# Attention and two FFNs on one core: attention by blocks of 256 tokens, in an order planned task by task

## The chip, the core and the metric

The kernel runs on one core of a Trainium2 chip. Its time is the device time of one execution in microseconds (us). The core has five engines with a queue of their own each: TensorE (PE, its weight loads shown as PEld), VectorE (DVE), ScalarE (ACT), GpSimd (POOL) and SyncE (SP), whose queue issues most DMAs. An engine works through its queue in order; what it needs from another engine it waits for at the instruction concerned.

## What is computed

Attention over 2 batches, 8 heads, 768 tokens and heads of 64, then two FFNs on the 1536 x 512 result, all in float32:

```python
scores = scale * np.matmul(q, k.transpose(0, 1, 3, 2))
is_sink = pos[None, :] < int(n_sink)                  # n_sink = 4
rel = pos[:, None] - pos[None, :]
in_window = (rel >= 0) & (rel < int(window))          # window = 128
scores = np.where(is_sink | in_window, scores, -1000000000.0)
a = np.exp(scores - np.max(scores, axis=-1, keepdims=True))
x = np.matmul(a / (np.sum(a, axis=-1, keepdims=True) + 1e-09), v)   # then (B, H, S, D) -> (B*S, H*D)
h = x @ w_in                                          # FFN 0: 512 -> 2048
g = np.where(h >= 1, h, np.where(h <= -1, 0.0, (h + 1) ** 2 / 4))
x = g @ w_out                                         # 2048 -> 512
h = x @ moe2_w_in                                     # FFN 1
out = np.maximum(h, 0.0) ** 2 @ moe2_w_out
```

The weights arrive as 64-bit floats and are turned into 32-bit numbers by bit operations on the chip.

## The kernel before

**Attention.** A unit of work (`UNITS`, L36) is a batch `b`, a block `j` of 256 tokens and a pair `c` of heads: 2 x 3 x 4 = 24 units. Because of the window, a unit needs the keys of its own block and, for j > 0, the last 128 keys of the block before and the 4 sink keys. Its steps are: load q, k, v for two pairs (`Loads.load`); copy the block-before keys by DMA on SP and the sink keys on POOL (`keys_before`); transpose k and q on PE and copy them out on DVE (`turn`); scores on PE for 128 rows of both heads, then mask, scale and minimum on DVE, then the exponential with its sum on ACT (`scores`, twice, `u` = 0 and 1); the reciprocal on DVE and the product with it on POOL, and for j > 0 the sink columns on POOL (`norm`); transposes of the weights on PE, copied by ACT (`turn_p`, twice; `turn_s` for the sink columns); the products with the values on PE, and the result split into a rounded high part (ACT) and the rest (DVE) in `x` (`values_of`).

**The FFNs.** Each product is done as three fp32r matmuls (`SPLIT`: high x high, high x low, low x high). The 2048 hidden columns of an FFN are 16 chunks of 128. A pass (`PASSES`, from `CUTS`, L48) holds two to four chunks; a step is one pass over some tokens: per chunk 12 matmuls for the hidden values (`hidden`, L175) and the activation on ACT, DVE and POOL, then four outputs of three matmuls per chunk (`outs`, L209), which DVE adds to an accumulator (L232, L234). A weight chunk comes in two halves (`part`, L121 to L130): two instructions on ACT, four on DVE, one on ACT, one on POOL, with one temporary buffer. Converted chunks stand in a ring of nine, six of which exist while attention runs.

**Order.** The order of `UNITS` is batch, then two pairs, then the three blocks of tokens, then the pairs. Each step of a unit has a number in `ORDER` (L44): unit index plus that number is its place in one list, which `fast_path` sorts. Into the same list go the weight conversions (`JOBS`), fillers on PE (`warm_pe`) and six FFN steps of 256 tokens (`STEPS`, L47): three of pass 0 (two chunks), three of pass 1 (three chunks). The scheduler of the language then picks, for each engine, what its model of time finds ready, with the list as priority. Behind attention its buffers are given to three more weight chunks, more hidden buffers (`G1`) and more PSUM banks, and the steps go on with 512 tokens (256 where a rest is left), always with the next conversions between the pieces (`Plan.job`).

Of the kernel before, what the change touches and what calls it, by code (L numbers as in the profile page):

```python
# [17 lines left out]
P = 128  # L18
# [14 lines left out]
AGAIN = 5, 2, 2, 2, 2, 2, 2, 2, 2, 1, 1, 1, 1, 1, 1, 1, 1  # L33
VB, KB = 3, 4
# [6 lines left out]
RING, EARLY = 9, 6  # L41
G0, G1 = 4, 6
LINE, BOTTOM, TOP = 2048, 26656, 229344
PSF, SCB, TPB, TXB, AVB = 2, 1, 1, 2, 1  # L44
JOBS = [4.00, 4.01, 4.50, 4.51, 5.05, 5.06, 5.58, 5.59, 6.63, 6.64, 6.81, 6.82, 7.15, 7.16, 7.67, 7.68, 8.20, 8.21, 8.44, 8.45, 8.68, 8.69, 9.47, 9.48]
ORDER = dict(
    q=-1.149, k=-2.190, v=-1.001, s0=-0.630, s1=0.512, t=-0.860, n=0.752, x0=1.240, xs=1.996, x1=1.174, a=2.080,  # L47
)  # L48
STEPS = [(13.70, (0, 0, 256)), (13.50, (0, 256, 256)), (17.60, (0, 512, 256)), (21.70, (1, 0, 256)), (21.20, (1, 256, 256)), (22.00, (1, 512, 256))]
CUTS = ((0, 2, 5, 8, 12, 16), (0, 4, 8, 12, 16))  # L50
# [6 lines left out]
def f32(ap):  # L57
    return ap.bitcast(F32)

# [27 lines left out]
class Weights:  # L87
# [20 lines left out]

    def part(self, key, h, tmp):
        nc, r = self.nc, self.raw.pop((key, h))  # L110
        if h == 0:
            pool = self.ring[self.turn % len(self.ring)]
            self.turn += 1
            self.split[key] = pool.tile([P, 2, 2 * E], F32R, tag="w", name=f"w_{key[0]}_{key[1]}")
        w = self.split[key][:, :, h * E : (h + 1) * E]
        nm = f"{key[0]}_{key[1]}_{h}"
        x = tmp.tile([P, E], F32, tag="wx", name=f"wx_{nm}")
        y = tmp.tile([P, E], F32, tag="wy", name=f"wy_{nm}")
        xi, yi = x.bitcast(I32), y.bitcast(I32)
        lo, hi = r[:, :, 0], r[:, :, 1]  # L120
        nc.scalar.activation(x, f32(hi), AF.Abs, scale=65536.0)  # L121
        nc.scalar.activation(yi, lo.bitcast(U32), AF.Copy, scale=2.0**-29)  # L122
        nc.vector.tensor_scalar(x, x, 2.0, None, ALU.max)  # L123
        nc.vector.tensor_scalar(xi, xi, 3, None, ALU.logical_shift_left)  # L124
        nc.vector.scalar_tensor_tensor(  # L125
            xi, hi, -(1 << 31), xi, ALU.bitwise_and, ALU.bitwise_or
        )
        nc.vector.tensor_tensor(xi, xi, yi, ALU.add)  # L128
        nc.scalar.copy(w[:, 0], x)  # L129
        nc.gpsimd.tensor_tensor(w[:, 1], x, f32(w[:, 0]), ALU.subtract)  # L130


class Ffn:
# [28 lines left out]
    def hidden(self, st, i):  # L162
# [3 lines left out]
        w = self.weights.split[key]  # L166
        x = self.x
        sl = slice(st["off"], st["off"] + nt)
        if i == 0:
            st["g"] = []  # L170
        h = self.bank(f"h_{nm}")[:, :nt]
        n = 0
        for c in range(4):
            for a, b in SPLIT:
                nc.tensor.matmul(  # L175
                    h, w[:, a, c * P : (c + 1) * P], x[:, b, c, sl], start=n == 0, stop=n == 11
                )
                n += 1
        g = po["g"].tile([P, 2, nt], F32R, tag="g", name=f"g_{nm}")
        u = po["tmp"].tile([P, nt], F32, tag="u", name=f"u_{nm}")  # L180
        if ffn == 0:
            t = po["tmp"].tile([P, nt], F32, tag="t", name=f"t_{nm}")
            nc.scalar.activation(u, h, AF.Relu, bias=self.half, scale=0.5)  # L183
            nc.vector.scalar_tensor_tensor(t, u, 1.0, u, ALU.min, ALU.mult)  # L184
            nc.vector.tensor_tensor(u, h, t, ALU.max)  # L185
            nc.scalar.copy(g[:, 0], u)  # L186
            nc.gpsimd.tensor_tensor(g[:, 1], u, f32(g[:, 0]), ALU.subtract)  # L187
        else:
            t = po["tmp"].tile([P, nt], F32, tag="t", name=f"t_{nm}")
            nc.scalar.activation(u, h, AF.Relu)  # L190
            nc.vector.scalar_tensor_tensor(t, h, 0.0, u, ALU.max, ALU.mult)  # L191
            nc.scalar.copy(g[:, 0], t)  # L192
            nc.gpsimd.tensor_tensor(g[:, 1], t, f32(g[:, 0]), ALU.subtract)  # L193
        st["g"].append(g)

    def outs(self, st, ob, part=slice(0, E)):
        nc = self.nc
        ffn, off, nt, chunks = st["ffn"], st["off"], st["nt"], st["chunks"]
        width = nt if ffn == 0 else part.stop - part.start
        o = self.bank(f"o_{st['nm']}_{ob}")[:, :width]  # L200
        n, m = 0, 3 * len(chunks)
        for key, g in zip(chunks, st["g"]):
            w = self.weights.split[key]
            for i, j in SPLIT:
                if ffn == 0:
                    lhs, rhs = w[:, i, E + ob * P : E + (ob + 1) * P], g[:, j, :]
                else:
                    lhs, rhs = g[:, i, ob * P : (ob + 1) * P], w[:, j, E:][:, part]
                nc.tensor.matmul(o, lhs, rhs, start=n == 0, stop=n == m - 1)  # L209
                n += 1  # L210
# [35 lines left out]
class Plan:  # L246
# [3 lines left out]
    def __init__(self, ffn, weights, wtmp):  # L250
# [11 lines left out]
        self.at = 0  # L262
# [68 lines left out]
class Attention:  # L331
# [17 lines left out]
    def sinks(self, b):  # L349
        nc, v = self.nc, self.loads.src["v"]  # L350
        raw = self.po["pt"].tile([P, 512], F32, tag="pt", name=f"vsr_{b}")
        raw = raw[:96].rearrange("p (h d) -> p h d", h=H)
        vs = self.po["vs"].tile([96, H, D], F32R, tag="vs", name=f"vs_{b}")
        nc.gpsimd.memset(raw, 0.0)
        for base in (0, 32, 64):
            for e in range(2):
                nc.sync.dma_start(
                    raw[base + e * NS : base + (e + 1) * NS, e::2, :],
                    v[b, e::2, 0:NS, :].rearrange("h t d -> t h d"),
                )  # L360
        nc.vector.tensor_copy(vs, raw)
        nc.vector.tensor_tensor(vs[64:96], raw[64:96], f32(vs[64:96]), ALU.subtract)
        self.vs[b] = vs

    def keys_before(self, b, j, c):
        nc = self.nc
        kt = self.po["k"].tile([P, 5, SLOT], F32, tag="k", name=f"k_{b}_{j}_{c}")
        if j > 0:
            old = self.kt[b, j - 1, c]
            nc.sync.dma_start(kt[:, 0, :P], old[:, 2, :P])  # L370
            nc.gpsimd.tensor_copy(
                kt[:, 0:2, P:], old[:, 1, P:].unsqueeze(1).broadcast_to([P, 2, NS])
            )
        self.kt[b, j, c] = kt

    def turn(self, b, j, c):
        nc, po, kt = self.nc, self.po, self.kt[b, j, c]
# [12 lines left out]
        for i in range(banks):  # L390
            blocks = slice(4 * i // banks, 4 * (i + 1) // banks)
            nc.vector.tensor_copy(kt[:, 1:, :P][:, blocks], ps[i][:, blocks])
        if j == 0:
            nc.gpsimd.tensor_copy(kt[:, 1, P:], kt[:, 1, :NS])
        self.st[b, j, c] = dict(nm=f"{b}_{j}_{c}")

    def scores(self, b, j, c, u):
# [6 lines left out]
        ps = [banks[:, e, :wid] for e in range(2)]  # L404
# [5 lines left out]
        if u == 0:  # L410
            st["p"] = [
                po["p"].tile([P, 2, WIN], F32, tag="p", name=f"p_{st['nm']}_{i}") for i in range(2)
            ]
            st["sm"] = po["sm"].tile([P, 3, 2, 2], F32, tag="sm", name=f"sm_{st['nm']}")
        s, sm = st["p"][u][:, :, :wid], st["sm"]
        mask = self.masks[min(2 * j + u, 2)][:, :wid]
        for e in range(2):
            nc.vector.tensor_tensor_reduce(  # L418
                s[:, e], ps[e], mask, -SCALE, 3.0e38, ALU.add, ALU.min, sm[:, 0, u, e : e + 1]
            )  # L420
        for e in range(2):
            nc.scalar.activation(  # L422
# [4 lines left out]
    def norm(self, b, j, c):  # L427
        nc, st = self.nc, self.st[b, j, c]
        sm = st["sm"]
        nc.vector.tensor_scalar(sm[:, 1], sm[:, 1], 1.0e-9, None, ALU.add)  # L430
        nc.vector.reciprocal(sm[:, 2], sm[:, 1])  # L431
        if j > 0:
            st["sp"], st["stt"] = self.sink_p[c % 2], self.sink_t[c % 2]
        for u in range(2):
            wid = P if j + u == 0 else WIN
            s = st["p"][u][:, :, :wid]
            r = sm[:, 2, u].unsqueeze(2).broadcast_to([P, 2, wid])
            nc.gpsimd.tensor_tensor(s, s, r, ALU.mult)  # L438
# [388 lines left out]
```

## Time and profile before

| | |
|---|---|
| runs, median (lowest to highest) | 666.81 us (665.79 to 667.2), 3 runs |
| the profiled execution | 669.3 us; span from first to last instruction 667.5 us |
| mean granted clock of PE in it | 0.994 |
| busy, of the span | PE 645.5, DVE 425.1, ACT 324.4, POOL 296.1 us |
| first score matmul, last value pass done | 8.93 us, 173.3 us |
| last matmul begun or running until | 662.7 us |

A matmul's end in the profile is modelled; the distance between the starts of two neighbours is what it cost where they stand close. An engine's idle time counts only where the chain of waits runs through it. Granted clock 1.00 is 2.4 GHz, 0.50 is 1.2 GHz.

### The profile page before, as it was taken

Reading aid. Unit: us, or ns where it says so; the run is one execution under the profiler, and the core shown is the slowest. Engines: PE = TensorE matmul, PEld = TensorE weight load, DVE = VectorE, ACT = ScalarE, POOL = GpSimd, SP = SyncE. Lnnn points to the kernel's source line nnn. Section 1 sums busy time; section 2 is a strip of 40 time slices with the busy share of each in tenths; the row PEclk is TensorE's granted clock in tenths of the full one; section 3 lists DMA queues with packets and bytes.
Section 4 is the critical chain, followed back from the end, with each engine's and each line's share of the span. In section 5 each row is a group of like instructions: output and inputs, shape, how many; then the busy total and the mean of one; then the engine's idle time right before and its main releaser. Section 6 shows DMA issues by size and latency. Waiting matters only on the chain.

```text
span 667.5 us, 9576 instructions
## 1 busy us (share of the span) xinstructions
PE 645.5 (97%) x3400; PEld 524.7 (79%) x3400; DVE 425.1 (64%) x885; ACT 324.4 (49%) x702; POOL 296.1 (44%) x302
## 2 busy tenths in 40 slices
PE   8888999999999999999999999999999999999997
PEld 7554677888888888877888878888888888888886
DVE  5688898966488887867776865664566356222221
ACT  2688877665454545445545554453444354122110
POOL 1365667546053535354346576353335343233111
PEclk9999899999999999999999989999999999999999
DMA  4846453110322222232312221321123020000111
GB/s 106 212 123 168 118 136 96 25 36 1 127 64 66 93 78 81 64 93 66 95 64 64 63 64 32 95 80 47 54 72 95 32 64 1 0 1 0 64 63 70
DMA packets 64345, 47.95 MB, mean 72 GB/s; under 512 B 40096, under 2 KB 58784, under 8 KB 64288
## 3 DMA queue, kind: packets, MB, share of 16 engines
q1 hardware_dynamic: 63456, 46.72, 24.1%
q8 instruction: 29, 0.48, 0.3%
q10 hardware_dynamic: 832, 0.52, 0.2%
q14 instruction: 28, 0.23, 0.1%
HBM read 43.04 MB, written 3.15 MB: 69 GB/s over the span
## 4 chain that ended last, share of the span: by engine, by line
PE 45%; DVE 5%; POOL 2%; ACT 2%; issue 1%; POOLq 0%; DVEq 0%
PE o L209 24%; PE h L175 21%; DVE t L184 1%; POOL x L220 1%; DVE wx L125 1%; POOL g L187 1%; DVE u L185 1%; POOL w L130 1%; DVE wx L123 1%; DVE wx L128 1%; DVE wx L124 0%; ACT u L183 0%; ACT g L186 0%; ACT wx L121 0%; ACT wy L122 0%
## 5 line engine op out<-in xcount | busy, mean ns | idle before, releaser
L175 PE MATMUL h<-x,w 128*128 128x512 f32 (+1 forms) x1272 | 272.7, 371 | 0.0
L175 PEld LDWEIGHTS h<-x,w 128*128 128x128 f32 x1272 | 223.8, 188 | 43.4 <-issue 1.2
L209 PE MATMUL o<-g,w 128*128 128x512 f32 (+1 forms) x696 | 143.8, 359 | 3.8 <-POOL g L187 2.0
L130 POOL TENSOR_TENSOR w<-wx,w 128x512 fp32r<-128x512 f32 x64 | 83.1, 1299 | 141.0 <-ACT w L129 133.5
L209 PEld LDWEIGHTS o<-g,w 128*128 128x128 f32 x696 | 116.6, 190 | 27.2 <-POOL g L187 3.9
L209 PE MATMUL o<-w,g 128*128 128x512 f32 (+1 forms) x588 | 132.7, 385 | 0.0
L209 PEld LDWEIGHTS o<-w,g 128*128 128x128 f32 x588 | 108.9, 188 | 22.1
L193 POOL TENSOR_TENSOR g<-t,g 128x512 fp32r<-128x512 f32 x48 | 64.1, 1335 | 100.5 <-ACT g L192 84.0
L234 DVE TENSOR_TENSOR acc<-o,acc 128x512 f32<-128x512 f32 (+1 forms) x105 | 58.3, 578 | 53.7 <-PE o L209 53.7
L187 POOL TENSOR_TENSOR g<-u,g 128x512 fp32r<-128x512 f32 (+1 forms) x58 | 69.0, 1192 | 52.7 <-ACT g L186 26.4
L129 ACT CAST w<-wx 128x512 fp32r<-128x512 f32 x64 | 39.9, 624 | 106.1 <-DVE wx L128 88.6
L123 DVE TENSOR_SCALAR wx<-wx 128x512 f32<-128x512 f32 x64 | 39.1, 611 | 60.9 <-ACT wx L121 60.7
L191 DVE SCALAR_TENSOR_TENSOR t<-h,u 128x512 f32<-128x512 f32 x48 | 33.1, 689 | 60.6 <-ACT u L190 34.4
L438 POOL TENSOR_TENSOR p<-p,sm 128x520 f32<-128x520 f32 (+1 forms) x48 | 49.5, 1052 | 44.5 <-DVE sm L431 44.5
L190 ACT ACTIVATE u<-h 128x512 f32<-128x512 f32 x48 | 28.6, 596 | 63.4 <-PE h L175 63.3
L125 DVE SCALAR_TENSOR_TENSOR wx<-wraw,wx 128x512 int32<-128x512 int32 x64 | 58.2, 910 | 1.2
L121 ACT ACTIVATE wx<-wraw 128x512 f32<-128x512 f32 x64 | 42.7, 668 | 32.3 <-POOL w L130 26.9
L422 ACT ACTIVATE p<-p,sm 128x260 f32<-128x260 f32 (+1 forms) x96 | 46.9, 491 | 22.5 <-DVE sm L418 22.4
L184 DVE SCALAR_TENSOR_TENSOR t<-u 128x512 f32<-128x512 f32 (+1 forms) x58 | 42.0, 726 | 18.6 <-ACT u L183 18.4
L128 DVE CUSTOM_DVE_ANT_0 wx<-wx,wy 128x1024 uint16<-128x1024 uint16 x64 | 50.1, 783 | 1.0
L122 ACT ACTIVATE wy<-wraw 128x512 int32<-128x512 uint32 x64 | 42.8, 668 | 6.9 <-DVE wx L128 6.9
L186 ACT CAST g<-u 128x512 fp32r<-128x512 f32 (+1 forms) x58 | 31.6, 546 | 27.9 <-DVE u L185 27.1
(72 smaller groups left out, 561.7 us busy)
## 6 DMA issues: line engine op xcount, KB each, us to landing
wraw<-in_moe_w_in_dram SPq DMA_DIRECT2D x32, 512.0 KB, 3.6
wraw<-in_moe_w_out_dram SPq DMA_DIRECT2D x32, 512.0 KB
vr<-in_v_dram SPq DMA_DIRECT2D x24, 128.0 KB, 2.3
qr<-in_q_dram SPq DMA_DIRECT2D x22, 128.0 KB, 2.8
kr<-in_k_dram SPq DMA_DIRECT2D x22, 128.0 KB, 2.8
out_dram<-acc SPq DMA_DIRECT2D x10, 256.0 KB, 2.0
k<-k SPq DMA_DIRECT2D x16, 64.0 KB, 2.5
qr<-in_q_dram SPq DMA_DIRECT2D x4, 64.0 KB
```

Of the source, the lines that this page charges most:

```text
L123: nc.vector.tensor_scalar(x, x, 2.0, None, ALU.max)
L125: nc.vector.scalar_tensor_tensor(xi, hi, -(1 << 31), xi, ALU.bitwise_and, ALU.bitwise_or)
L128: nc.vector.tensor_tensor(xi, xi, yi, ALU.add)
L130: nc.gpsimd.tensor_tensor(w[:, 1], x, f32(w[:, 0]), ALU.subtract)
L175: nc.tensor.matmul(h, w[:, a, c * P : (c + 1) * P], x[:, b, c, sl], start=n == 0, stop=n == 11)
L184: nc.vector.scalar_tensor_tensor(t, u, 1.0, u, ALU.min, ALU.mult)
L187: nc.gpsimd.tensor_tensor(g[:, 1], u, f32(g[:, 0]), ALU.subtract)
L193: nc.gpsimd.tensor_tensor(g[:, 1], t, f32(g[:, 0]), ALU.subtract)
L209: nc.tensor.matmul(o, lhs, rhs, start=n == 0, stop=n == m - 1)
L234: self.nc.vector.tensor_tensor(dst, o, dst, ALU.add)
L422: nc.scalar.activation(s[:, e], s[:, e], AF.Exp, bias=sm[:, 0, u, e : e + 1], scale=-1.0, accum_out=sm[:, 1, u, e : e + 1],)
L438: nc.gpsimd.tensor_tensor(s, s, r, ALU.mult)
```

## The change

- `UNITS` now runs batch, block, pair: all four pairs of 256 tokens stand together, and a block's predecessor is four units back.
- Every step of attention, of the weight conversion and of the FFN steps is cut into functions that issue instructions of one engine each (`keys_load`, `keys_sink`, `turn`, `turn_copy`, `scores`, `least`, `powers`, `norm`, `weigh`, `sink_cols`, `turn_p`, `turn_p_copy`, `turn_s`, `turn_s_copy`, `turn_s_low`, `values_of`, `rows_high`, `rows_low`; `parts`; `hidden_parts`, `out_parts`). The instructions themselves are the same. A hidden product is two tasks of six matmuls that begin when all four pairs are there.
- A `Planner`, run when the program is built, simulates the engines with a price per kind of task (`COST`) and gives each task a time: always the task that can start first, and among equals the lowest key (`KEYS`, `STEPS`, `LOADS`, `PARTS`). The tasks are issued in that order within `manual_schedule()`, which keeps each engine's order inside the region; where later instructions fall among them stays the scheduler's.
- Ten FFN steps of 256 tokens are in the plan instead of six, of passes of three chunks each: `CUTS` of FFN 0 becomes (0, 3, 6, 10, 13, 16). Pass 2 then holds chunks 6 to 9. Six chunks are converted in the plan, as before.
- Fillers on PE go into gaps of the plan ahead of the first FFN matmul only (`warm_gaps`).
- Buffers: v 5 instead of 3, keys 6 instead of 4, hidden 7 instead of 4, both accumulators at fixed places; the room comes from a smaller scratch for DMA descriptors (`DMA_SCRATCH`).

```diff
-UNITS = [
-    (b, j, g * GRP + c)
-    for b in range(B) for g in range(NC // GRP) for j in range(3) for c in range(GRP)
+UNITS = [(b, j, c) for b in range(B) for j in range(3) for c in range(NC)]
-STEPS = [(13.70, (0, 0, 256)), (13.50, (0, 256, 256)), (17.60, (0, 512, 256)), (21.70, (1, 0, 256)), (21.20, (1, 256, 256)), (22.00, (1, 512, 256))]
-CUTS = ((0, 2, 5, 8, 12, 16), (0, 4, 8, 12, 16))
+STEPS = [
+    (0, 0, 10.09), (0, 256, 12.27), (1, 0, 9.77), (0, 512, 3.39), (1, 256, 14.42),
+    (0, 768, 18.80), (1, 512, 19.48), (0, 1024, 24.08), (1, 768, 42.06), (1, 1024, 21.07),
+]
+CUTS = ((0, 3, 6, 10, 13, 16), (0, 4, 8, 12, 16))
+START = 8700.0
+LAG = dict(PE=53, ACT=33, DVE=33, POOL=78, SP=40)
+COST = dict(
...
+    e=("ACT", 994, 1100, 0), es=("ACT", 780, 880, 0), xc=("ACT", 492, 587, 0), xxc=("ACT", 375, 467, 0),
...
+class Planner:
...
+    def run(self):
...
+        while len(order) < len(self.tasks):
+            best = None
+            for e, tasks in ready.items():
+                for t in tasks:
+                    at = self.starts(t, free)
+                    if at is not None:
+                        c = (max(at, idle[e]), t.key, t)
+                        if best is None or c[:2] < best[:2]:
+                            best = c
...
+            order.append(t)
...
+def warm_gaps(order, nc, ident, psf):
+    out, last, begun = [], START, False
+    for t in order:
+        if t.engine == "PE":
+            begun = begun or t.kind in ("mm", "m1")
+            count = int((t.start - last - 250) / 225)
+            if count > 0 and not begun:
+                out.append(lambda n=len(out), c=count: warm_pe(nc, ident, psf, f"c{n}", c))
+            last = t.start + t.step
+        out.append(t.emit)
+    return out
...
-            for _, _, f, args in sorted(events, key=lambda ev: ev[:2]):
-                if f == calls["s0"] and args == UNITS[0]:
-                    with tc.manual_schedule(engines={mybir.EngineType.DVE}):
-                        f(*args)
-                        masks.rest()
-                else:
-                    f(*args)
-            plan.flush()
+            at.mask_rest = masks.rest
+            with tc.manual_schedule():
+                order = fast_plan(at, ffn, weights, plan.stage, plan.wtmp)
+                for emit in warm_gaps(order, nc, at.ident, psf):
+                    emit()
```

## Rows read from the trace of the kernel before

**Rows 1.** The page, part 1: engine, busy us (share of the span) x instructions.

```profile
PE 645.5 (97%) x3400; PEld 524.7 (79%) x3400; DVE 425.1 (64%) x885; ACT 324.4 (49%) x702; POOL 296.1 (44%) x302
```

**Rows 2.** Windows: stretch, length, busy us by engine, granted clock, DMA share, GB/s.

```profile
core 0: us, PE busy (x) PEld busy (x) DVE busy (x) ACT busy (x) POOL busy (x), PEclk, DMA share, GB/s
...
9.00:40.80 31.80, 26.77 (x198) 18.91 (x198) 22.61 (x85) 20.42 (x66) 11.27 (x21) 1.00 0.65 163
40.80:100.00 59.20, 53.08 (x399) 37.42 (x397) 52.49 (x166) 47.96 (x142) 37.23 (x54) 0.97 0.56 143
100.00:173.30 73.30, 72.08 (x582) 58.88 (x580) 53.41 (x164) 46.92 (x139) 39.80 (x57) 1.00 0.14 37
...
395.60:662.70 267.10, 267.06 (x1181) 221.23 (x1181) 122.45 (x184) 96.33 (x164) 98.37 (x75) 0.99 0.14 46
```

**Rows 3.** The chain of waits, late: start us, us, what.

```profile
406.83 10.88 PE h L175 x48
```

**Rows 4.** Groups from 9 to 173.3 us: busy us, mean ns; idle before.

```profile
L407 PE MATMUL s<-k 64*128 64x260 f32 (+1 forms) x192 | 33.1, 417 | 6.6 <-DVE sm L418 5.8 <-DVE k L392 0.5 <-issue 0.2
L453 PE MATMUL tx<-ident,p 128*128 128x128 f32 x176 | 30.0, 283 | 1.3 <-POOL p L438 0.9 <-DMA wraw<-in_moe_w_in_dram 0.3
L175 PE MATMUL h<-x,w 128*128 128x256 f32 (+1 forms) x181 | 27.4, 295 | 0.0
L209 PE MATMUL o<-g,w 128*128 128x256 f32 x180 | 27.3, 294 | 1.0 <-DVE acc L232 0.8 <-DVE u L185 0.2
...
L491 PE MATMUL av<-pt,vr 128*64 128x128 f32 (+1 forms) x256 | 24.8, 326 | 1.6 <-ACT pt L457 0.8 <-DVE x L494 0.7
...
L385 PE MATMUL tp<-ident,kr 128*128 128x128 f32 x46 | 10.3, 296 | 0.4 <-DMA kr<-in_k_dram 0.4
...
L184 DVE SCALAR_TENSOR_TENSOR t<-u 128x256 f32<-128x256 f32 x15 | 7.9, 537 | 4.1 <-ACT u L183 4.0
...
L185 DVE TENSOR_TENSOR u<-h,t 128x256 f32<-128x256 f32 x15 | 6.2, 419 | 0.5
```

**Rows 5.** Timeline of PE, 100 to 215 us: start, us, instruction, count.

```profile
151.92 0.28 PE L491 MATMUL av<-sink_t,vs 96*128 96x256 f32 x1
152.13 1.09 PE L491 MATMUL av<-pt,vr 128*64 128x256 f32 x12
153.15 0.66 PE L453 MATMUL tx<-ident,p 128*128 128x128 f32 x4
153.56 1.08 PE L209 MATMUL o<-g,w 128*128 128x256 f32 x7
154.57 0.71 PE L407 MATMUL s<-k 64*128 64x260 f32 x4
155.21 0.65 PE L453 MATMUL tx<-ident,p 128*128 128x128 f32 x4
...
157.09 2.40 PE L209 MATMUL o<-g,w 128*128 128x256 f32 x18
159.33 0.28 PE L491 MATMUL av<-sink_t,vs 96*128 96x256 f32 x1
```

**Rows 6.** Timeline of PE, 0 to 60 us.

```profile
40.79 0.60 PE L175 MATMUL h<-x,w 128*128 128x256 f32 x3
```

**Rows 7.** Timeline of ACT, 0 to 45 us.

```profile
23.48 0.37 ACT L493 CAST x<-av 128x256 fp32r<-128x256 f32 x1
```

**Rows 8.** Timeline of POOL, 160 to 310 us; 17 like rows of L130 lie between.

```profile
182.38 1.30 POOL L130 TENSOR_TENSOR w<-wx,w 128x512 fp32r<-128x512 f32 x1 [15.60 <-ACT w L129]
...
305.55 1.30 POOL L130 TENSOR_TENSOR w<-wx,w 128x512 fp32r<-128x512 f32 x1
```

**Rows 9.** Timeline of the DMA queue SP, 120 to 310 us.

```profile
173.40 0.37 SPq L101 DMA_DIRECT2D wraw<-in_moe_w_in_dram  x1
```

**Rows 10.** Windows in the thin stretch; columns as in rows 2.

```profile
65.00:70.00 5.00, 3.20 (x18) 1.88 (x19) 4.11 (x16) 4.81 (x15) 3.19 (x4) 0.88 0.39 112
70.00:72.00 2.00, 2.00 (x11) 1.59 (x11) 1.43 (x7) 1.57 (x6) 1.05 (x4) 0.50 0.00 0
```

More of the change, by code (lines that the diff above doesn't have):

```diff
@@ L58, in f32, with __init__, add, starts @@
     return ap.bitcast(F32)
+class Hold:
+    def __init__(self, pool):
+        self.pool, self.left, self.end = pool, 0, 0.0
+class Task:
+    def __init__(self, kind, key, emit, after, takes, uses):
+        self.kind, self.key, self.emit = kind, key, emit
+        self.engine, self.step, self.took, self.extra = COST[kind]
+        self.after = [t for t in after if t is not None]
+        self.takes, self.uses = takes, uses
+        self.next = []
+        self.start = self.end = None
+class Planner:
+    def __init__(self, slots, start):
+        self.slots, self.begin, self.tasks = slots, start, []
+    def add(self, kind, key, emit, after=(), takes=(), uses=()):
+        t = Task(kind, (key, len(self.tasks)), emit, after, list(takes), list(uses))
+        for h in t.uses:
+            h.left += 1
+        for d in t.after:
+            d.next.append(t)
+        self.tasks.append(t)
+        return t
+    def starts(self, t, free):
+        at = t.ready
+        need = {}
+        for h in t.takes:
+            need[h.pool] = need.get(h.pool, 0) + 1
+        for pool, n in need.items():
+            if len(free[pool]) < n:
+                return None
+            at = max(at, sorted(free[pool])[n - 1] + LAG[t.engine])
+        return at
+    def run(self):
+        free = {pool: [0.0] * n for pool, n in self.slots.items()}
+        ready = {e: [] for e in LAG}
+        idle = {e: self.begin for e in LAG}
+        dma, gps = self.begin, [(0.0, 0.0)]
+        for t in self.tasks:
+            t.wait, t.ready = len(t.after), self.begin
+            if not t.wait:
+                ready[t.engine].append(t)
+        order = []
+        while len(order) < len(self.tasks):
[7 more added lines that the diff above has]
+                            best = c
+            assert best, [(e, [t.kind for t in tasks]) for e, tasks in ready.items()]
+            at, _, t = best
+            ready[t.engine].remove(t)
+            step, took = t.step, t.took
+            if t.engine == "DVE" and t.extra:
+                more = sum(max(0.0, min(b, at + took) - max(a, at)) for a, b in gps[-3:]) * t.extra
+                step, took = step + more, took + more
+            t.start = at
+            idle[t.engine] = at + step
+            if t.engine == "SP":
+                dma = max(at + step + 900, dma) + t.extra
+                t.end = dma + 1100
+            else:
+                t.end = at + took
+            if t.engine == "POOL":
+                gps.append((at, t.end))
+            for h in t.takes:
+                free[h.pool].remove(min(free[h.pool]))
+            for h in t.uses:
+                h.left -= 1
+                h.end = max(h.end, t.end)
+                if not h.left:
+                    free[h.pool].append(h.end)
+            order.append(t)
+            for x in t.next:
+                x.wait -= 1
+                same = x.engine == t.engine and t.engine != "SP"
+                lag = (0 if t.engine == "PE" else 34) if same else LAG[x.engine]
+                end = t.start + t.step if same and t.engine == "PE" else t.end
+                x.ready = max(x.ready, end + lag)
+                if not x.wait:
+                    ready[x.engine].append(x)
+        return order
@@ L196, in outs, with hidden, out_parts @@
+        return ops + [("gc", high), ("gl", low)]
+    def hidden(self, st, i):
+        for _, f in self.hidden_parts(st, i):
+            f()
+    def out_parts(self, st, ob):
+        n = len(st["chunks"])
+        s = {}
+        return [
+            ("mm", lambda a=a: self.out_mm(st, ob, slice(0, E), a, min(a + 2, n), s))
+            for a in range(0, n, 2)
+        ] + [("ad", lambda: self.out_add(st, ob, slice(0, E), s["o"]))]
     def outs(self, st, ob, part=slice(0, E)):
+        s = {}
+        self.out_mm(st, ob, part, 0, len(st["chunks"]), s)
+        self.out_add(st, ob, part, s["o"])
@@ L197, in outs, with out_mm @@
+    def out_mm(self, st, ob, part, lo, hi, s):
         nc = self.nc
-        ffn, off, nt, chunks = st["ffn"], st["off"], st["nt"], st["chunks"]
+        ffn, nt, chunks = st["ffn"], st["nt"], st["chunks"]
         width = nt if ffn == 0 else part.stop - part.start
[L200 to L203, printed above, removed]
+        if lo == 0:
+            s["o"] = self.bank(f"o_{st['nm']}_{ob}")[:, :width]
+        for n in range(lo, hi):
+            w, g = self.weights.split[chunks[n]], st["g"][n]
@@ L261, in __init__ @@
         self.left = [NT] * len(PASSES)
-        self.at = 0
+        for ps, _, _ in STEPS if begun else ():
+            self.left[ps] -= HALF
+        self.at = 4 * EARLY if begun else 0
         self.pend = []
@@ L349, in sinks @@
     def sinks(self, b):
[L350 to L360, printed above, removed]
@@ new lines, in fast_plan @@
+def fast_plan(at, ffn, weights, stage, wtmp):
+    line = Planner(SLOTS, START)
+    units = at.plan(line)
+    plan_ffn(line, ffn, weights, stage, wtmp, units)
+    return line.run()
+def warm_gaps(order, nc, ident, psf):
[9 more added lines that the diff above has]
+    return out
```

525 lines of the change are left out of this document (353 added, 172 removed).

## The prediction

> **What bounds the kernel now.** I read the page's busy times first, then the stages as windows, then the order on TensorE, then the instruction groups of the attention stage. TensorE (PE) is busy for 97% of the span [rows 1], so only time in which PE is badly filled can be won. The windows say where that is [rows 2]: from 395.6 to 662.7 us PE is busy without a break, and the chain there runs through matmuls alone, 48 of 512 columns in 10.88 us, 0.2267 us each [rows 3]. From 9.0 to 173.3 us, the attention stage, the three windows show 5.0, 6.1 and 1.2 us of open idle time. The rest of the bad filling is hidden in "busy", because the modelled end of a matmul covers short waits. So I price PE's own work there by start-to-start intervals in dense places [rows 5]: a score step (four passes) takes 0.64 us (154.57 to 155.21), a transpose of 128 columns 0.41/4 = 0.1025 us (153.15 to 153.56), a pass of the values 1.02/12 = 0.085 us with 0.21 us for the sink part before it, and an FFN matmul of 256 columns 2.24/18 = 0.1244 us (157.09 to 159.33). With the counts of the stage [rows 4]:
>
> - scores: 192/4 = 48 steps x 0.64 = 30.7 us
> - transposes: 176 of the weights, 2 x 46 of k and q, 32 of the sink columns (16 blocks x 2): 300 x 0.1025 = 30.8 us
> - values: 256 x 0.085, and 16 blocks with a sink part x 0.21 = 25.1 us
> - FFN: 361 x 0.1244 = 44.9 us
>
> Together 131.5 us of 164.3. So 32.8 us are gaps, fillers that only keep the clock up, and changes from one kind of work to another. That sum is what the change can shrink.
>
> **The change part by part.** *Moved work.* Steps of 256 tokens in the stage go from six (2+2+2+3+3+3 = 15 chunk passes) to ten of three chunks (30). A chunk pass is 12 + 12 matmuls, so 360 more of 256 columns enter: 360 x 0.1244 = 44.8 us. They leave the later stage, where they were 180 of 512 columns: 180 x 0.2267 = 40.8 us [rows 3]. The move alone costs 4.0 us. The remainder behind the stage holds 144 instead of 120 matmuls of 256 columns, at most 24 x (0.1244 - 0.1133) = 0.3 us. Thus the time changes by 4.3 us plus the change of the gaps.
>
> *What fills the gaps.* In the old unit order two head pairs run through three blocks of tokens before the next two start, so the first 256 tokens have all four pairs only after eight units. The first FFN matmul starts at 40.79 us [rows 6], and its group of twelve is strung out behind the pairs as they come. In the new order four units without a previous block finish 256 tokens. The first unit's x was written at 23.48 us [rows 7]. A unit of this kind costs PE 0.41 + 1.28 + 0.62 + 0.68 = 3.0 us by the prices above. Three more behind the first, at about that pace and with weights to be converted beside them, put the first FFN matmul at 33 to 36 us (an estimate from these rows). Until then PE has some five units' work, 15 us in 26, so 11 us of gap stay. From there a step or two of FFN belong to each four units, and the two last steps need nothing of attention. For the other 150 us or so I take 5% of gap: between the 2% that the window from 100 us shows openly and the 10% of the one before it [rows 2], nearer to the first as the mix of work is like that one's. That is 7.5 us. Sum: 18.5 us of gap instead of 32.8. Bounds: 10 us, if only the beginning stays open; 33 us, if the plan brings nothing.
>
> *Other engines.* VectorE (DVE) has 128.5 us of busy time in the stage [rows 2]. It gets 15 more of each of two instructions at 0.537 and 0.419 us [rows 4] and 16 more additions, priced as the latter: 21 us. 150 us in a stage of 190 to 200 us do not bind on average; in the first 60 us, where three chunks are converted beside nine units, they nearly do, and this is why I leave gaps there. ScalarE (ACT) has 115.3 us and gets 30 instructions priced likewise, under 16 us; GpSimd (POOL) 88.3 us and 15 more. Neither comes near.
>
> *Split tasks and fixed order.* The same instructions are issued, so the split itself costs nothing unless an engine's fixed order meets a late input. Then everything behind it on that engine waits. Before, such a wait showed in small pieces only. I put its price into the 5% and keep it for the range. Larger buffer counts (v, k, g) and the second accumulator in its own place add no instruction. Their cover is PE's own work; if it is gone, the waits count as gaps. The DMA queue of SP issues as many loads as before in the stage, in another order; the k copies between blocks now lie four units apart instead of two, which takes a wait away rather than adding one.
>
> *Behind the stage.* Six weight chunks are ready in both kernels. Before, the stage left 768 tokens of passes 0 (two chunks) and 1 (three): 5 x 768 tokens, 180 x 0.2267 = 41 us, until pass 2 needed chunks 5 to 7. Now 256 tokens of three and three chunks remain, 144 x 0.1244 = 18 us, and pass 2 needs chunks 6 to 9, none of them ready. A part (half a chunk) took 6.84 us in the old kernel: 19 one after another from 182.38 to 305.55 us, 18 distances [rows 8]. Chunk 9's first half is the seventh part, 48 us after the start of conversions. PE reaches it after 18 + 3 x 12 x 0.2267 = 26 us. So at that pace conversions must begin some 22 us before the planned part ends. The old kernel's first load of these came at 173.40 us, with the end of attention [rows 9]; the planned order holds only among its own instructions, so later ones may slip in as soon as buffers are free. The last two steps of the plan are FFN alone, 144 matmuls, 18 us. At the old pace that is 4 us short, but half as wide steps leave DVE and ACT more room beside the conversions; I count no stall.
>
> The sum: 4.3 + 18.5 - 32.8 = -10.0 us. The profiled execution took 669.3 us (span 667.5 and 1.8 around it), 2.5 above the median of the runs, 666.8. So 659.3 in its terms and 657 in those of the median.
>
> *A rule against the change.* Between 65 and 72 us, PE with small gaps, the granted clock fell to 0.88 and 0.50 [rows 10], 0.50 being 1.2 instead of 2.4 GHz. The changed kernel puts fillers only ahead of its first FFN matmul. The Trainium skill ("TensorE: Matmul & The Clock Gate", Part 1: The HAM clock gate) says that the low clock is the default and that activity lifts it; by that rule the trace agrees, and gaps between 35 and 60 us would be run at the lower level. This is the third rival below.
>
> **The rivals.** *Weights late (slower).* If conversions of chunks 6 to 9 begin only when the planned part is over, PE waits 48 - 26 = 22 us: 679 us. It decides from the point at which fewer than about 12 us of FFN are left on PE when the first conversion starts, since then a stall of 10 us eats the gain. For it: conversions went one after another in the old trace, each part behind the one before [rows 8]. Against it: attention's buffers come free before the last two steps.
>
> *The gaps stay.* A fixed order made from prices meets other durations on the chip and waits elsewhere: with 29 us of gap, 4.3 + 29 - 32.8 = +0.5, so 667 us. For it: in the first windows ACT and DVE are busy for 64 to 89% of the time [rows 2], so the chain of a unit, not PE, sets the pace. Against it: the window from 100 us already reached 98% with the same mix.
>
> *The clock falls early.* At 0.50 the 12 value passes and the like take up to twice their time; over 5 us of PE work in the thin stretch that is 5 us more: 662 us. For it the two windows named, against it the earlier FFN matmuls.
>
> *More is won.* Gaps of 10 us: 4.3 + 10 - 32.8 = -18.5, so 648 us. For it: little but the beginning is bound by anything but PE.
>
> **How the numbers follow.** Chances: forecast 0.45 (650 to 662), weights late 0.18, gaps stay 0.12, clock 0.08, more won 0.17. Likeliest: 657 us. The range goes from 647 (just beyond more won) to 670 (over half of the stall of late weights), leaving out about 0.1 at either end. About 0.2% is what a measurement can tell from no change: faster, under 665.5, takes the forecast, more won, the clock and a little of gaps stay, 0.72; within it 0.08; slower 0.20.
>
> **What would show it.** Right: the first FFN matmul at 33 to 36 us; the last planned FFN matmul near 204 us (9.0 + 86.6 of attention + 89.6 + 18.5) and the last value pass some 18 us before it; 720 matmuls of 256 columns before that point; PE without a gap of over 1 us where pass 2 begins; behind the stage 48 matmuls per 10.88 us as before. Wrong: PE waiting for the weights' POOL line some 20 us behind the planned part; PE idle for 5 us or more in any 20 us after 60 us; a granted clock under 0.9 between 35 and 60 us; the first FFN matmul after 40 us.

## The result, and the profile after

The changed kernel takes 671.1 us (median of 4 runs, 670.45 to 672.18), the kernel before 666.94 (4 runs, 665.79 to 667.2): 1.0067 times as long, 95% interval 1.0047 to 1.0087. So it is slower by 0.5 to 0.9%, where -10 us was forecast, and outside the range of 647 to 670.

The profiled execution took 670.47 us (span 668.7). First the page's busy times, against [rows 1]:

```profile
PE 642.5 (96%) x3576; PEld 532.4 (80%) x3576; DVE 434.0 (65%) x909; ACT 326.6 (49%) x718; POOL 297.0 (44%) x310
```

The windows, cut where the work changes (columns as in [rows 2]):

```profile
9.00:36.70 27.70, 24.67 (x182) 16.86 (x180) 21.88 (x82) 19.14 (x65) 12.62 (x22) 1.00 0.83 203
36.70:100.00 63.30, 59.38 (x469) 43.35 (x467) 58.97 (x191) 54.10 (x163) 40.68 (x62) 1.00 0.58 148
100.00:185.30 85.30, 84.39 (x691) 73.69 (x689) 56.79 (x162) 48.27 (x135) 39.32 (x55) 1.00 0.06 18
185.30:237.00 51.70, 49.19 (x363) 46.22 (x362) 39.24 (x79) 27.08 (x54) 23.26 (x23) 1.00 0.32 103
237.00:410.50 173.50, 173.50 (x766) 143.32 (x764) 137.19 (x207) 87.62 (x149) 89.26 (x71) 1.00 0.24 76
410.50:419.00 8.50, 0.04 (x2) 0.04 (x1) 5.26 (x8) 4.72 (x9) 5.54 (x5) 0.79 0.17 62
419.00:424.00 5.00, 5.00 (x15) 4.04 (x16) 4.31 (x6) 2.77 (x6) 3.01 (x3) 0.67 0.32 92
424.00:429.50 5.50, 5.50 (x26) 4.53 (x25) 3.88 (x7) 1.62 (x4) 2.20 (x2) 1.00 0.15 43
```

The stage is denser, as forecast. There is one place that the forecast did not have: 8.5 us at 410.5 in which PE does nothing at all, and 5 us behind it at a granted clock of 0.67. PE's timeline shows the first FFN matmul [rows 6], the last values, the small waits behind them (L354 is the last step of FFN 0's activation ahead of `g`, L417 the addition to the accumulator) and the stop:

```profile
36.68 0.96 PE L326 MATMUL h<-x,w 128*128 128x256 f32 x6
...
184.24 1.09 PE L701 MATMUL av<-pt,vr 128*64 128x256 f32 x12
...
206.52 1.31 PE L387 MATMUL o<-g,w 128*128 128x256 f32 x9 [1.21 <-DVE u L354]
...
211.00 5.66 PE L387 MATMUL o<-g,w 128*128 128x256 f32 x45 [0.20 <-DVE acc L417]
216.50 1.60 PE L326 MATMUL h<-x,w 128*128 128x256 f32 x12
...
408.30 2.20 PE L387 MATMUL o<-w,g 128*128 128x512 f32 x9
418.96 10.68 PE L387 MATMUL o<-w,g 128*128 128x512 f32 x39 [8.46 <-ACT g L346]
429.48 5.83 PE L326 MATMUL h<-x,w 128*128 128x512 f32 x25
```

The same place before, by PE's timeline of that kernel, had 1.7 us of waits:

```profile
393.95 0.50 PE L209 MATMUL o<-g,w 128*128 128x512 f32 x1 [0.49 <-ACT g L186]
395.62 11.21 PE L209 MATMUL o<-g,w 128*128 128x512 f32 x41 [1.18 <-POOL g L187]
```

PE waits for `g` of ACT. ACT's timeline shows why it is late (L402 splits a new x, L271, L254 and L250 convert weights, L335 and L346 are the activation of the product that PE waits for):

```profile
409.63 0.61 ACT L402 CAST x<-acc 128x512 fp32r<-128x512 f32 x1
410.56 0.67 ACT L250 ACTIVATE wx<-wraw 128x512 f32<-128x512 f32 x1 [0.32 <-POOL w L272]
411.13 0.60 ACT L402 CAST x<-acc 128x512 fp32r<-128x512 f32 x1
414.07 0.62 ACT L402 CAST x<-acc 128x512 fp32r<-128x512 f32 x1 [2.34 <-DVE acc L417]
415.45 0.62 ACT L271 CAST w<-wx 128x512 fp32r<-128x512 f32 x1 [0.76 <-DVE wx L270]
415.98 0.66 ACT L254 ACTIVATE wy<-wraw 128x512 int32<-128x512 uint32 x1
416.54 0.58 ACT L335 ACTIVATE u<-h 128x512 f32<-128x512 f32 x1
...
418.31 0.60 ACT L346 CAST g<-t 128x512 fp32r<-128x512 f32 x1
```

ACT is not full: it works 4.72 of the 8.5 us. The activation stands in its queue behind x splits and conversions that themselves wait, for the additions and conversion steps on DVE. The order comes from `Plan.step`: it issues as many hidden products as there are free buffers (`ahead`), then the outputs of the step before, then the rest. The change of `CUTS` gives FFN 0 a last pass of three chunks. With six buffers, three of FFN 1's first four products go ahead of these outputs; the fourth comes behind them, and behind the four x splits that the last step of FFN 0 brings. PE, in its turn, has only two products of the next step and nine output matmuls (33 matmuls, 7.5 us) to do until it needs the fourth: that product was done at 402.9 us, a third of the 36 matmuls from 400.14 on, and its activation began at 416.54.

**The ledger**, with the prediction's prices. A matmul of 256 columns behind the stage costs (216.50 - 211.00)/45 = 0.122 us. By 185.3 us 541 of them are done:

```profile
L326 PE MATMUL h<-x,w 128*128 128x256 f32 x289 | 41.2, 290 | 0.2 <-DVE u L354 0.2
L387 PE MATMUL o<-g,w 128*128 128x256 f32 x252 | 35.3, 290 | 0.1
```

- Gaps of the stage: 185.3 - 9.0 - 86.6 of attention - 541 x 0.1244 = 22.4 us, before 32.8: **-10.4**.
- FFN work: 541 x 0.1244 + 324 x 0.122 + 1872 x 0.2267 = 531.2 us, before 361 x 0.1244 + 120 x 0.122 + 2064 x 0.2267 = 527.5: **+3.7**.
- What is left behind the stage, waits and low clock: 663.7 (PE's end) - 185.3 - 39.5 - 424.4 = 14.5 us, before 662.7 - 173.3 - 14.6 - 467.9 = 6.9: **+7.6**.

The sum, +0.9, is PE's end, 1.0 us later. The medians differ by 4.2, since the profiled execution of before was 2.4 us above its median, and that of after 0.6 below. Which of the three terms these 3.2 us belong to is not shown.

### The profile page after: what moved, and what is told of

The parts are those of the page before. It is cut to its first block, busy times and chain, and to the rows that moved or that the text cites. A ratio compares the mean times of both kernels' runs of the same rounds, so it can differ in the third digit from the quotient of the medians.

```text
span 668.7 us, 9971 instructions
## 1 busy us (share of the span) xinstructions
PE 642.5 (96%) x3576; PEld 532.4 (80%) x3576; DVE 434.0 (65%) x909; ACT 326.6 (49%) x718; POOL 297.0 (44%) x310
## 4 chain that ended last, share of the span: by engine, by line
PE 83%; DVE 8%; ACT 5%; POOL 1%; issue 1%; DMA 1%; DVEq 0%; ACTq 0%; POOLq 0%
PE o L387 38%; PE h L326 35%; PE av L701 3%; PE s L608 3%; PE tx L660 2%; PE tp L583 1%; ACT p L629 1%; DVE wx L260 1%; DVE wx L267 1%; DVE p L620 1%; DVE wx L270 1%; POOL w L272 1%; DVE k L596 1%; ACT wx L250 1%; DVE t L340 1%
## 5 line engine op out<-in xcount | busy, mean ns | idle before, releaser
L326 PE MATMUL h<-x,w 128*128 128x512 f32 (+1 forms) x1368 | 276.4, 357 | 0.5 <-DVE u L354 0.4
L326 PEld LDWEIGHTS h<-x,w 128*128 128x128 f32 x1368 | 229.6, 189 | 41.0 <-DVE u L354 2.4
L387 PE MATMUL o<-g,w 128*128 128x256 f32 (+1 forms) x792 | 142.8, 334 | 2.3 <-DVE u L354 1.8
L387 PE MATMUL o<-w,g 128*128 128x512 f32 (+1 forms) x588 | 134.5, 388 | 8.5 <-ACT g L346 8.5
L387 PEld LDWEIGHTS o<-g,w 128*128 128x128 f32 x792 | 121.8, 189 | 19.5 <-ACT w L271 1.4
L350 POOL TENSOR_TENSOR g<-u,g 128x256 fp32r<-128x256 f32 (+1 forms) x66 | 70.7, 1073 | 83.0 <-ACT g L346 54.3
L417 DVE TENSOR_TENSOR acc<-o,acc 128x512 f32<-128x512 f32 (+1 forms) x109 | 59.2, 562 | 55.5 <-PE o L387 55.3
L271 ACT CAST w<-wx 128x512 fp32r<-128x512 f32 x64 | 39.8, 621 | 99.8 <-DVE wx L270 86.1
L342 DVE SCALAR_TENSOR_TENSOR t<-h,u 128x512 f32<-128x512 f32 x48 | 33.1, 689 | 64.7 <-ACT u L335 38.4
L267 DVE TENSOR_SCALAR wx<-wx 128x512 f32<-128x512 f32 x64 | 37.5, 585 | 44.0 <-ACT wx L250 43.8
L340 DVE SCALAR_TENSOR_TENSOR t<-u 128x256 f32<-128x256 f32 (+1 forms) x66 | 47.7, 722 | 25.3 <-ACT u L333 25.0
L335 ACT ACTIVATE u<-h 128x512 f32<-128x512 f32 x48 | 28.5, 594 | 63.8 <-PE h L326 63.8
L260 DVE SCALAR_TENSOR_TENSOR wx<-wraw,wx 128x512 int32<-128x512 int32 x64 | 57.7, 902 | 1.2
L250 ACT ACTIVATE wx<-wraw 128x512 f32<-128x512 f32 x64 | 42.8, 668 | 24.0 <-POOL w L272 21.8
L333 ACT ACTIVATE u<-h,half 128x256 f32<-128x256 f32 (+1 forms) x66 | 37.2, 567 | 32.1 <-PE h L326 30.4
L346 ACT CAST g<-u 128x256 fp32r<-128x256 f32 (+1 forms) x66 | 33.1, 503 | 31.1 <-DVE u L354 27.8
```

Of the source, the lines that this page charges most:

```text
L250: nc.scalar.activation(s["x"], f32(s["r"][:, :, 1]), AF.Abs, scale=65536.0)
L260: nc.vector.scalar_tensor_tensor(s["xi"], s["r"][:, :, 1], -(1 << 31), s["xi"], ALU.bitwise_and, ALU.bitwise_or)
L267: ("c1", lambda: nc.vector.tensor_scalar(s["x"], s["x"], 2.0, None, ALU.max)),
L326: nc.tensor.matmul(s["h"], w[:, a, c * P : (c + 1) * P], x[:, b, c, sl], start=n == 0, stop=n == 11)
L340: nc.vector.scalar_tensor_tensor(t, s["u"], 1.0, s["u"], ALU.min, ALU.mult)
L350: nc.gpsimd.tensor_tensor(g[:, 1], s["u" if ffn == 0 else "t"], f32(g[:, 0]), ALU.subtract)
```

## The experiments

The first four were chosen when the stop at 410 had been seen, but not its cause.

**Earlier values and weights.** The first load of chunk 6 is issued at 185.37 us, with the last value product, as in the kernel before [rows 9]. This run lets it come earlier.

```diff
-"av" if j else "avv", key("av"), at(self.values_of), turned + [d["v"]], [av],
+"av" if j else "avv", key("av") - (8.0 if n > 19 else 0.0), at(self.values_of), turned + [d["v"]], [av],
```

> The keys of the last four units' value products are 8 lower, so that the last of them stands ahead of the 72 output matmuls that it followed (it ran at 184.0 us). Theory A, the weights of pass 2 are late because these products hold the buffers: the first load of chunk 6 moves from 185.4 to about 174 us, the 4.5 us that PE lost between 196 and 237 us go, and the stop at 410 us stays: 666 to 667 us. Rival, conversions are late because other engines are full there: the load moves but PE still loses 4 us, 671 us.

679.8 us (678.02 to 680.33), above both forecasts. The load came at 175.39, ten us earlier, and the time went up by 8.7 us. PE now waits all along the planned tail, in its timeline:

```profile
197.04 0.95 PE L387 MATMUL o<-g,w 128*128 128x256 f32 x6 [0.88 <-DVE u L354]
...
426.91 11.97 PE L387 MATMUL o<-w,g 128*128 128x512 f32 x39 [8.31 <-ACT g L346]
```

Late weights are not the cause of the stop: with earlier ones it is the same, 8.31 us.

**Other cuts.** FFN 0's last pass gets four chunks again, as before.

```diff
-CUTS = ((0, 3, 6, 10, 13, 16), (0, 4, 8, 12, 16))
+CUTS = ((0, 3, 6, 9, 12, 16), (0, 4, 8, 12, 16))
```

> Passes of FFN 0 are 3, 3, 3, 3, 4 chunks instead of 3, 3, 4, 3, 3. Theory A (the stop of 8.5 us at 410 us and the 1.7 us of low clock behind it come with a last pass of three chunks): the stop shrinks to the 2 to 4 us of the old kernel; pass 2 waits for three chunks instead of four, so the loss at 200 to 220 us shrinks too: 661 to 665 us. Rival (the stop comes from conversions queued between the last outputs, whatever the cut): stop of 6 us or more stays, 667 to 670 us.

669.25 us (668.77 to 670.19), 1.9 under the changed kernel; the intervals just overlap (1.0025 to 1.005 against 1.0047 to 1.0087). The time is the rival's, but the one stop is gone, as the rival did not have it; smaller ones stand in its place, 1.34 us at 346, 1.65 at 368 to 370 and, at FFN 1's start:

```profile
393.63 0.50 PE L387 MATMUL o<-g,w 128*128 128x512 f32 x1 [0.38 <-ACT g L346]
395.17 1.66 PE L387 MATMUL o<-g,w 128*128 128x512 f32 x6 [1.03 <-POOL g L350]
397.93 8.29 PE L387 MATMUL o<-g,w 128*128 128x512 f32 x35 [1.10 <-ACT g L346]
```

So where passes of three and four chunks meet changes the place and size of the stop.

**No conversions between the last outputs of FFN 0.**

```diff
-            self.job()
+            if st["ffn"] or not st["last"] or st["off"] + st["nt"] < NT:
+                self.job()
```

> Behind the last four outputs of FFN 0 no conversion is queued; they follow later. Rival theory (conversions between these outputs delay the activation of FFN 1's fourth hidden product): the stop at 410 us falls from 8.5 to under 3 us, 662 to 664 us. Theory A (the length of the pass makes it): the stop stays above 6 us, 669 to 671 us.

671.86 us (671.11 to 672.23), stop 8.48 us. This tells nothing: the scheduler put the conversions into the same places of ACT's queue all the same.

**Without the fixed order.** The same plan is issued, but later instructions and the scheduler's own choice may reorder it.

```diff
-            with tc.manual_schedule():
+            with ExitStack():
```

> The planned list is only a priority; the scheduler of the language may order the stage's instructions. If the fixed order brings the gain inside the stage (22.4 us of gap instead of 32.8), the stage gets longer by 5 us or more: 675 us or above. Rival, the fixed order itself makes waits: the stage gets shorter, 666 to 669 us.

685.3 us (684.26 to 687.06), as expected: the same plan without its fixed order costs 14 us more. PE is busy for 21.87 us of the first window, where the changed kernel has 24.67, and the stop is there too (8.23 us at 435.12).

**One buffer more, and two.** Now the theory was the order in ACT's queue.

```diff
-G0, G1 = 7, 6
+G0, G1 = 7, 7      # in the second run 7, 8
```

> One more buffer for hidden products behind the attention stage (G1 = 7 for 6), nothing else. Theory (order): the stop of 8.46 us at 410.5 is there because only three of the four hidden products of FFN 1's first step find a buffer ahead of the outputs of FFN 0's last step, so that the fourth one's activation stands behind their four x splits; with seven buffers all four go ahead, the stop falls below 2 us, the 1.7 us of low clock behind it go too, and the time is 660 to 663 us, under before's 666.9. Rival (load): ACT, DVE and POOL are simply full there with x splits and weight conversions; then the stop stays over 5 us, as it did in three other arrangements, and the time is 669 to 672 us.

> Two more buffers (G1 = 8). By the order theory the second one adds little: with seven, four hidden products already fit behind a pass of three chunks; steps behind a pass of four still get only three ahead with seven and four with eight, and no stall was read there. So the same time as with seven, within 0.5 us. By the rival (load) 669 to 672 us again.

With seven 670.3 us (669.59 to 671.66), with eight 660.19 (659.76 to 661.67; 0.9892 of before, interval 0.9873 to 0.9911). Neither came as the theory had it: seven gave the rival's time, and the step to eight everything. With seven, the stop at 410 is gone as expected, but a new one stands one step later, in PE's timeline of that run:

```profile
421.66 11.04 PE L326 MATMUL h<-x,w 128*128 128x512 f32 x48
432.54 2.20 PE L387 MATMUL o<-w,g 128*128 128x512 f32 x9
441.61 1.22 PE L387 MATMUL o<-w,g 128*128 128x512 f32 x2 [6.87 <-ACT g L346]
```

There the step before has four chunks, so that three products go ahead of its outputs and the fourth is last again: by `Plan.step` it comes behind these outputs, as the first twelve of the 48 matmuls at 421.66. From 427.7 us on only conversions stand ahead of its activation in ACT's queue, the same run:

```profile
432.83 0.62 ACT L271 CAST w<-wx 128x512 fp32r<-128x512 f32 x1 [3.25 <-DVE wx L270]
...
438.39 0.62 ACT L271 CAST w<-wx 128x512 fp32r<-128x512 f32 x1 [2.88 <-DVE wx L270]
...
439.48 0.58 ACT L335 ACTIVATE u<-h 128x512 f32<-128x512 f32 x1
```

The product was done at about 424.4, and its activation began at 439.48, 15 us later; PE's cover, three products of the next step and nine output matmuls (45 matmuls), was 10.2 us. With eight buffers all four products of a step go ahead of the outputs of the step before, and the next step's four behind these, so that 84 to 96 matmuls (19 to 22 us) and the first nine of its own outputs lie between a step's last product and its use. ACT's queue is as crowded (the `u` of the first product of 404.39 runs at 421.56, 14 us after it, behind the same splits and conversions), but nothing waits for it, as these products are used from 437.03 on, in PE's timeline of that run:

```profile
404.39 11.04 PE L326 MATMUL h<-x,w 128*128 128x512 f32 x48
415.27 11.04 PE L387 MATMUL o<-w,g 128*128 128x512 f32 x48
...
437.03 11.04 PE L387 MATMUL o<-w,g 128*128 128x512 f32 x48
```

So the theory holds in its core (a product behind the outputs is late because of what stands in ACT's queue) and was too narrow: not the x splits of one place, but any product that comes last with little cover. The rival, that the engines are full there, falls: the same work fits without a wait.

**The smaller loss at 196 to 222 us.** PE waits there for the plan's last activations. One run leaves most of the conversions beside them out (one POOL copy for chunks 6 to 8); a second adds the earlier values to it.

```diff
     def part(self, key, h, tmp):
+        if key[0] == 0 and 6 <= key[1] <= 8:
...
+            r = f32(self.raw.pop((key, h))[:, :, 1])
+            self.nc.gpsimd.tensor_copy(w, r.unsqueeze(1).broadcast_to([P, 2, E]))
+            return
```

> As g7, but chunks 6 to 8 of FFN 0's weights aren't converted: after their load one copy on POOL (high word, to both halves) stands in for the eight conversion steps, so ACT's three and DVE's four steps of each of these six parts are left out and the output is not the reference's. If the 4.5 us of idle PE between 185.3 and 236.9 come from conversions that stand ahead of the last planned activations on ACT and DVE, this is 3 to 5 us under g7, and the waits of 1.2 and 0.6 us at 206 and 208 go. If they come from the plan's own chain through two PSUM banks, it is within 1 us of g7 and the waits stay.

> As g7n, with the earlier key for the value products of the last four units (the edit of e1_early_values, which cost 8.7 us there). If it was the conversions, let in 10 us earlier, that made that edit dear, it costs under 2 us here or gains up to 2 us against g7n. If the new order of PE itself was dear, it costs 6 to 9 us here as well.

668.73 us (667.41 to 670.07) and 674.32 (673.65 to 674.66), each between its two forecasts. The waits stayed, as chunk 9's conversion moved up into the place; the 1.6 us under the run with seven buffers are not theirs, since the later stop is shorter here (4.00 us at 439.46 for 6.87). DVE's timeline of the first of these runs shows one product's two steps (L349, L363) between four conversion steps; PE waited 1.96 us for it:

```profile
202.22 0.83 DVE L267 TENSOR_SCALAR wx<-wx 128x512 f32<-128x512 f32 x1
203.09 0.87 DVE L268 TENSOR_SCALAR wx<-wx 128x512 int32<-128x512 int32 x1
203.99 0.69 DVE L260 SCALAR_TENSOR_TENSOR wx<-wraw,wx 128x512 int32<-128x512 int32 x1
204.60 0.42 DVE L349 SCALAR_TENSOR_TENSOR t<-u 128x256 f32<-128x256 f32 x1
204.94 0.68 DVE L270 CUSTOM_DVE_ANT_0 wx<-wx,wy 128x1024 uint16<-128x1024 uint16 x1
205.54 0.42 DVE L363 TENSOR_TENSOR u<-h,t 128x256 f32<-128x256 f32 x1
```

The earlier values cost 5.6 us here instead of 8.7. Part of the difference is the stop: its low clock lasted longer in the earlier run. Up to the stop the cost is 416.40 - 408.30 = 8.1 us there and 438.96 - 433.26 = 5.7 here, so that at most some 2.4 us go with the conversions that were left out. The larger part is there without them; that PE's new order makes it is likely but not shown, as chunk 9's conversion came earlier too.

**With eight buffers: fewer planned steps, and chunks 6 to 9 without conversion.** The first run takes two steps out of the plan, the second extends the copy in place of conversion to chunk 9.

```diff
-    (0, 768, 18.80), (1, 512, 19.48), (0, 1024, 24.08), (1, 768, 42.06), (1, 1024, 21.07),
+    (0, 768, 18.80), (1, 512, 19.48), (0, 1024, 24.08),
```

```diff
-        if key[0] == 0 and 6 <= key[1] <= 8:
+        if key[0] == 0 and 6 <= key[1] <= 9:
```

> As g8 (660.2 us), with the last two FFN steps of the plan (pass 1 at tokens 768 and 1024) taken out of it; their 512 tokens go behind the stage, as one step 512 wide in eight banks. 144 matmuls of 256 columns become 72 of 512: 144 x 0.12 = 17.3 us for 72 x 0.2267 = 16.3. If the loss of 4.5 us between 185 and 237 us is the two-bank chain of those planned steps, most of it goes too: 655 to 658 us. Rival: the conversions of chunks 6 and 7 then stand in the way of the same products, and the work drawn out of the stage leaves PE short at its end: 660 to 664 us.

> As g8, but chunks 6 to 9 of FFN 0's weights get one copy on POOL in place of their conversion (the output is not the reference's). With seven buffers the same edit to chunks 6 to 8 drew chunk 9's conversion into the place of theirs, and a product waited 1.96 us behind its DVE steps; here none is left before 220 us. If conversions ahead of activations make the loss at 196 to 213 us (2.4 us of idle PE in g8), it falls under 0.8 us and the time is 1.5 to 3 us under g8's. If it is the chain of one product through two banks, it stays at 2 us or more and the time is within 1 us of g8's.

660.35 us (659.84 to 661.32): the loss only changed its place, to 2.29 us at 206.39 behind `ACT g`, so the rival's time came out. Without the conversions 659.1 us (659.05 to 659.55), with waits still there in PE's timeline:

```profile
202.55 3.14 PE L335 MATMUL h<-x,w 128*128 128x256 f32 x24 [0.37 <-DVE u L363]
...
210.93 5.65 PE L396 MATMUL o<-g,w 128*128 128x256 f32 x45 [0.85 <-DVE acc L426]
```

Together 1.7 us of waits instead of 2.5 with the conversions, and 1.1 us of time; the two intervals overlap (0.9856 to 0.9888 against 0.9873 to 0.9911). The time lies between the two forecasts. Conversions may be a part of this loss; what the rest is stays open.

**The kernel before with eight buffers.** To make room its ring of weight chunks has eight slots for nine; the changed kernel with the same ring is its partner.

```diff
-RING, EARLY = 9, 6
-G0, G1 = 4, 6      # the changed kernel: 7, 6
+RING, EARLY = 8, 6
+G0, G1 = 4, 8      # the changed kernel: 7, 8
```

> The kernel before with eight hidden buffers (G1 = 8) and, to make room, a ring of eight weight chunks for nine. If the four buffers too few are what cost it 2.1 us of stall and 1.9 of low clock at 391 to 400 us, it gains 2 to 4 us: 663 to 665 us; the change is then worth some 3 to 5 us where both have the buffers. Rival: the shorter ring delays conversions, and it is at 667 us or over.

> The partner of b8r8: the changed kernel with eight hidden buffers and a ring of eight. If the ninth chunk of the ring is of no weight in time, this is at g8's 660 us within 0.7; if it delays conversions, over 662 us, and b8r8 has to be read against this one.

The kernel before falls to 661.79 us (661.11 to 663.07; 0.9913, interval 0.9899 to 0.9927), more than I expected; PE's timeline shows no wait behind its attention stage. The changed one stands at 659.66 (659.48 to 659.83; 0.988, interval 0.9864 to 0.9897): the ring's ninth slot has no weight in time. With the buffers in both, the change is worth 2.1 us, 0.3%; the intervals do not overlap. That fits the ledger, taken from the changed kernel's own trace: -10.4 and +3.7 us, and 51.7 - 39.5 - 36 x 0.2267 = 4.0 us lost from 185.3 to 237 us, where the old kernel has no wait; -2.7 in all.

The fastest version that computes the whole is the changed kernel with eight hidden buffers, with either ring: 660 us, 1.1 to 1.2% under the kernel before.

## Why the prediction was wrong

**Nearly right: the start.** The first FFN matmul stands at 36.68 us, 0.7 behind the forecast's 33 to 36 (before 40.79 [rows 6]). By the prices 9.0 to 36.7 us hold 17.8 us of work and 9.9 of gap; forecast were 11.

**Right: the moved work.** 541 + 324 matmuls of 256 columns, +3.7 us against +4.3. The last value product was forecast for 18 us before 204, thus 186; it stands at 184.24. The last planned FFN matmul did not come near 204: it is the last of the 45 that begin at 211.00, and ends at 216.5. Some 48 matmuls of later steps slipped in between the plan's, and the small waits from 201 to 211 us lie ahead of it.

**Mis-sized: the 5% of gap behind the start.** From 36.7 to 185.3 us it is 11.9 us instead of 7.5. I took it as nearer to the 2% of the last of the old windows [rows 2], for all of the 150 us. That fits only the last part, where 2.8 of 85.3 us are gap. The middle has 9.1 of 63.3 us, 14%, by the count of its groups on PE:

```profile
L608 PE MATMUL s<-k 64*128 64x260 f32 (+1 forms) x88 | 14.7, 411 | 0.9 <-DVE sm L620 0.7
L326 PE MATMUL h<-x,w 128*128 128x256 f32 x84 | 13.0, 295 | 0.0
L660 PE MATMUL tx<-ident,p 128*128 128x128 f32 x85 | 13.0, 281 | 0.8 <-DVE sink_t L684 0.7
L701 PE MATMUL av<-pt,vr 128*64 128x128 f32 (+1 forms) x120 | 11.1, 320 | 0.0
L583 PE MATMUL tp<-ident,kr 128*128 128x128 f32 x24 | 5.0, 288 | 0.4 <-DVE k L596 0.3
L583 PE MATMUL tp<-ident,qr 128*128 128x128 f32 x24 | 4.6, 273 | 0.0
L673 PE MATMUL ts<-ident,sink_p 128*96 128x128 f32 x16 | 3.4, 282 | 1.6 <-ACT pt L667 1.0 <-POOL sink_p L648 0.6
L387 PE MATMUL o<-g,w 128*128 128x256 f32 x20 | 3.3, 295 | 0.1
L701 PE MATMUL av<-sink_t,vs 96*128 96x256 f32 x8 | 2.9, 361 | 0.3 <-DVE sink_t L684 0.3
```

(88 x 0.16 for scores, 149 transposes x 0.1025, 120 x 0.085 and eight sink parts x 0.21 for values, 104 x 0.1244: 54.2 us.) DVE is busy for 58.97 of these 63.3 us, 93%: I had written that it nearly binds there, and then took the share of a stretch where it does not. That DVE sets the pace is read from the busy share alone, not tested. In sum the gaps went from 32.8 to 22.4 us, -10.4 where I had -14.3.

**Wrong: "I count no stall" behind the stage.** This step failed, and it turned the sign. I asked only whether weights would be ready, for pass 2. They were: its products begin at 221.97 us without a gap of over 1 us. Chunk 9's first half was begun on POOL at 233.75, 44 us after the first conversion on ACT (189.54), where I had 48. But `CUTS` also changed what meets at FFN 1's start, a pass of three and a pass of four chunks with six buffers, and I never went through `Plan.step` with the new numbers. The price was 8.46 us of stop and 10.52 - 39 x 0.2267 = 1.7 of low clock behind it. The run with two buffers more takes it away and gives 660.2, 3 us over my 657; the mis-sized gaps are 3.9. A second loss behind the stage that I counted as nothing is the 4.0 us from 185.3 to 237 us, whose cause stays open in part. One of my own signs of being wrong came true here, PE idle for 5 us or more in any 20 us after 60 us.

**The baseline's own loss.** I took PE from 395.6 us on as full, and treated what lay between 173.3 and 395.6 as none of the change's business. The kernel before gains 5.5 us in its run with eight buffers (667.32 to 661.79), and its waits behind the stage are gone there. So of the 10.9 us that the buffers give the changed kernel, as much as half would have come without the change.

**The rivals.** Weights late: false, no wait for POOL's weights. The gaps stay: false, a third of them went. The clock early: false, the granted clock is 1.00 in all windows to 410 us; it fell later, behind the stop. More won: false. The slower side came by a mechanism that none of them had.

## What to carry to other kernels

Where a change alters how work is cut, go through every place where the new pieces meet with the program's own rule for how many go ahead of what; a product that comes last needs cover for all that stands in its activation's queue, not for the activation alone. Before a stage is made denser, give the kernel before the buffers that the new one might lack: here 5.5 of the 7.7 us between the kernel before and the fastest version (667.32, 661.79 and 659.66) came from the buffers alone. Take a gap share from a stretch in which the same engines are as full.

## What the runs showed of the hardware

- A stop of PE costs more than its length. Behind 8.46 us of idle PE the granted clock is 0.50 (1.2 GHz) from 419 to 422 us, 0.67 over 419 to 424, and 39 matmuls took 10.52 us for the 8.84 at full clock, 1.7 more. Behind the like stops of three other runs (8.31, 8.48 and 8.23 us: with earlier values, with no conversions between the last outputs, without the fixed order) they took 11.81, 11.75 and 10.88, thus 3.0, 2.9 and 2.0 more. In the run with eight buffers the same stretch has 1.00. The Trainium skill ("TensorE: Matmul & The Clock Gate", Part 1: The HAM clock gate) says that the low clock is the default and that activity lifts it; the trace agrees, 1.00 in the window from 424 us on, with PE busy throughout.
- Some DVE instructions take twice as long or more while POOL works. L268 in the changed kernel took 0.84 us at 395.59 beside a POOL instruction, and 0.41 at 404.09 alone; L260 at 424.44 of the run with eight buffers took 1.66 beside one of 1.42, and 0.68 at 418.98 alone. Others do not: L342 in the changed kernel took 0.69 at 400.51 beside a POOL instruction of 1.30, and 0.68 at 403.49 alone.
